# Transposing q and k unsplit, and splitting them as they leave PSUM

## The chip, the core and the metric

The kernel runs on one core of a Trainium2 chip. The metric is device time in microseconds, the median of several executions. One execution was also recorded by the profiler; its instruction times are what a reader of this document sees.

## What is computed

Attention with ALiBi-like distances under a mask (a local window of 96 keys and 8 global keys), for 4 batches, 8 heads, 768 positions and a head width of 64, and behind it a feed-forward block (512 to 2048 to 512) whose nonlinearity is a rational function.

```python
def _attn_ref(q, k, v, n_global, n_local):
    scale = 1.0 / np.sqrt(D)
    scores = scale * np.matmul(q, k.transpose(0, 1, 3, 2))
    rel = pos[:, None] - pos[None, :]
    is_global = pos[None, :] < int(n_global)
    is_local = (rel >= 0) & (rel < int(n_local))
    dist = np.where(is_global & ~is_local, float(n_local), np.abs(rel))
    slopes = 2.0 ** (-8.0 * (np.arange(H) + 1) / H)
    scores = scores - slopes[:, None, None] * dist
    scores = np.where(is_global | is_local, scores, -1000000000.0)
    a = softmax(scores)
    return np.matmul(a, v)

def _moe_ref(x, w_in, w_out, a, b):
    h = x @ w_in
    P = a[0] + a[1] * h + a[2] * h * h + a[3] * h * h * h
    Q = 1.0 + np.abs(b[0]) * np.abs(h) + np.abs(b[1]) * h * h
    return (P / (Q + 1e-06)) @ w_out
```

## The kernel before

**Work.** The attention is cut into 96 units (`NU`). A unit is one block of 128 queries of two neighbouring heads: `unit(u)` gives the chunk `c` of 256 tokens, the half `t`, the head pair `p`, the batch `b` and the block `i` of its sequence. Four units in a row have the same block and the four head pairs. Scores are taken over two key blocks, the query's own and the one before, in which the first 8 columns are overwritten with the global keys. The FFN is cut into 96 blocks `f`, each with two halves of the first matmul (`st_ffn1`, 12 matmuls a half), an elementwise chain over ScalarE, GpSimd and VectorE (`st_ew1` to `st_ew4`) and two halves of the second matmul (`st_ffn2`, 6 matmuls a half).

**Two precisions.** Up to unit 23 (`PLAIN = 24`) the scores are float32 matmuls. From unit 24 on each of q and k is split into a high part rounded to float32r and a low part, the rest, also float32r, and the score is taken with matmuls of float32r:

- `st_load` (L135 to L142): per two units, two DMAs on SyncE (SP) fetch 128 rows of four heads of q and of k into one tile `nat`, of which there are two.
- `st_split` (L382 to L388): VectorE copies q and k of the unit's two heads (256 columns in all) to float32r, the high part, and GpSimd subtracts it from the original, the low part. Both go to one tile `sp`, high and low of a head side by side.
- `st_qkT` (L390 to L405): four TensorE transposes of 128x128, one for each of q and k and each head, write one PSUM bank `tk`. Since high and low of one head (64 columns each) lie side by side, a transpose leaves the high part on partitions 0 to 63 and the low part on 64 to 127.
- `st_qkE` (L410 to L435): ScalarE takes q of each head to `qT` with the scale of the scores (a power of two that also holds the head's slope), and k of both heads to `kT`. Two SP DMAs of 64 KB exchange the halves of `qT`, giving a second copy with the low part above. In the first block of a sequence ScalarE also keeps the 8 global keys in `kG`.
- `st_score` (L437 to L466): for each head two matmuls of 128x128 by 128x256 into one bank `s`: with the straight `qT` (high by high and low by low) and with the exchanged one (high by low and low by high). GpSimd then puts the global keys into the first 8 columns of the k block; VectorE takes the scaled score with the mask to `pr` and finds its minimum.
- `st_soft`, `st_norm`, `st_pT`, `st_pv`, `st_x`: the exponentials (ScalarE), the normalization (GpSimd), four transposes of float32 into a bank `tp`, the product with v into a bank `o` for every two units, and its split into `xh` and `xl`, the FFN's input.

The tiles `tk`, `s`, `tp` and `o` share three PSUM banks (`ps_t`, `bufs=3`), asked for in the order of the program: within an iteration `s`, `tk`, `o` in odd iterations, `tp`. Accesses by different engines to a bank, and all other dependencies, are ordered by the tile framework with semaphores.

**Order.** A loop over `t` (L586 on) writes the steps of different units down together: the load of unit t+4, the scores of unit t-2, the transposes of unit t, the split of unit t+1, `pv` of the pair begun at t-5, the probabilities' transposes of unit t-3 and one FFN block. Each step has a priority, 1000 t plus a number from a table (`PRI`: score 50, soft 100, ffn1a 150, qkT 200, pv 250, qkE 300, split 400, ew3 450, ffn1b 550, ffn2a 750, pT 800, ffn2b 850). The framework's planner makes each engine's and each queue's fixed order from these priorities and from when, by its own model, an instruction is ready. At unit 24 the memory of the early tiles is given back and a pool `late` is opened in it.

Of the kernel before, what the change touches and what calls it, by code (L numbers as in the profile page):

```python
# [9 lines left out]
F32 = mybir.dt.float32  # L10
FR = mybir.dt.float32r
I32 = mybir.dt.int32
BF16 = mybir.dt.bfloat16
U16 = mybir.dt.uint16
AF = mybir.ActivationFunctionType
ALU = mybir.AluOpType
PSUM = bass.MemoryType.PSUM

P = 128
G = 8  # L20
# [14 lines left out]
PLAIN = 24  # L35
# [70 lines left out]
def tile_kernel(ctx: ExitStack, tc: tile.TileContext, q, k, v, n_global, n_local,  # L106
                w_in, w_out, ca, cb, out):
    nc = tc.nc
    B, H, S, D = q.shape
# [13 lines left out]
    pl = SimpleNamespace(tmps=TMPS, gbufs=GBUFS, split=False)  # L123


    nat = {}
    vts = {}

    def unit(u):
        c, j = divmod(u, UPC)  # L130
        t, p = divmod(j, NPAIR)
        b, i = divmod(2 * c + t, NT)
        return c, t, p, b, i

    def st_load(u):  # L135
        c, t, p, b, i = unit(u)
        hs = slice(2 * p, 2 * p + 4)
        r = slice(i * P, (i + 1) * P)
        n = pl.ldp.tile([P, 2, 4, D], F32, tag="nat", name=f"nat{u}")
        nc.sync.dma_start(out=n[:, 0], in_=q[b, hs, r, :].rearrange("h s d -> s h d"))  # L140
        nc.sync.dma_start(out=n[:, 1], in_=k[b, hs, r, :].rearrange("h s d -> s h d"))
        nat[u // 2] = n  # L142

    def st_load_v(u):
# [140 lines left out]
    def is_last(f):  # L285
        return f == NU - 1 and not pl.split
# [81 lines left out]
    ident = const.tile([P, P], F32, name="ident")  # L368
    ident_r = const.tile([P, P], FR, name="ident_r")
    mask0 = const.tile([P, P], BF16, name="mask0")  # L370
    masks = const.tile([P, 3, P], BF16, name="masks")
    sp = {}
    tqk = {}
# [5 lines left out]
    def blocks_of(x, i):  # L379
        return x if i else x[..., 0, :]  # L380

    def st_split(u):  # L382
        p = unit(u)[2]
        n = nat[u // 2][:, :, 2 * (p % 2):2 * (p % 2) + 2, :]
        s = pl.late.tile([P, 2, 2, 2, D], FR, tag="split", name=f"sp{u}", bufs=1)
        nc.vector.tensor_copy(out=s[:, :, :, 0, :], in_=n)  # L386
        nc.gpsimd.tensor_tensor(out=s[:, :, :, 1, :], in0=n, in1=s[:, :, :, 0, :], op=ALU.subtract)  # L387
        sp[u] = s  # L388

    def st_qkT(u):  # L390
        if u < PLAIN:
            p = unit(u)[2]
            tk = pl.ps_t.tile([P, 2, P], F32, tag="t", name=f"tk{u}")
            for z in range(2):
                n = nat[u // 2][:, z, 2 * (p % 2):2 * (p % 2) + 2, :]
                nc.tensor.transpose(out=tk[:, z, :], in_=n.rearrange("p a d -> p (a d)"), identity=ident)
            tqk[u] = tk
            return
        s = sp.pop(u)
        tk = pl.ps_t.tile([P, 2, 2, P], FR, tag="t", name=f"tk{u}")  # L400
        for z in range(2):
            for x in range(2):
                nc.tensor.transpose(out=tk[:, z, x, :], in_=s[:, z, x].rearrange("p a d -> p (a d)"),  # L403
                                    identity=ident_r)
        tqk[u] = tk  # L405


# [2 lines left out]
    def st_qkE(u):  # L410
        c, t, p, b, i = unit(u)
        tk = tqk.pop(u)
        hs = slice(2 * p, 2 * p + 2)
        if u < PLAIN:
            qz = pl.qz[:, u % 3]
            for x in range(2):
                ds_ = slice(x * D, (x + 1) * D)
                nc.scalar.activation(out=qz[ds_, x, :], in_=tk[ds_, 0, :], func=AF.Copy,
                                     scale=float(2.0 ** (2 * p + x - 2)))
            nc.scalar.copy(out=pl.kF[:, p, i % 2, :], in_=tk[:, 1, :])  # L420
            if i == 0:
                nc.scalar.copy(out=pl.kGF[:, p, :], in_=tk[:, 1, 0:G])
            qTs[u] = qz
            return
        kT, kG = pl.kT, pl.kG
        qT = pl.late.tile([P, 2, 2, P], FR, tag="qT", name=f"qT{u}", bufs=2)
        for x in range(2):

            nc.scalar.activation(out=qT[:, 0, x], in_=tk[:, 0, x], func=AF.Copy, scale=float(2.0 ** (2 * p + x - 2)))
        nc.sync.dma_start(out=qT[0:D, 1].bitcast(F32), in_=qT[D:P, 0].bitcast(F32))  # L430
        nc.sync.dma_start(out=qT[D:P, 1].bitcast(F32), in_=qT[0:D, 0].bitcast(F32))
        nc.scalar.copy(out=kT[:, hs, i % 2, :], in_=tk[:, 1])
        if i == 0:
            nc.scalar.copy(out=kG[:, hs, :], in_=tk[:, 1, :, 0:G])
        qTs[u] = qT  # L435

    def st_score(u):  # L437
        c, t, p, b, i = unit(u)
        qT = qTs.pop(u)
        s_ps = pl.ps_t.tile([P, 2, 2, P], F32, tag="t", name=f"s{u}")  # L440
        for x in range(2):
            h = 2 * p + x
            if u < PLAIN:
                nc.tensor.matmul(out=blocks_of(s_ps[:, x], i), lhsT=qT[:, x, :], rhs=blocks_of(pl.kF[:, p], i),  # L444
                                 start=True, stop=True)
                continue
            rhs = pl.kT[:, h] if i else pl.kT[:, h, 0:1, :].broadcast_to([P, 2, P])
            for z in range(2):
                nc.tensor.matmul(out=s_ps[:, x], lhsT=qT[:, z, x, :], rhs=rhs, start=(z == 0), stop=(z == 1))  # L449
        if 1 <= i < NT - 1 and u < PLAIN:  # L450
            nc.gpsimd.tensor_copy(out=pl.kF[:, p, i % 2, 0:G], in_=pl.kGF[:, p, :])
        elif 1 <= i < NT - 1:
            hs = slice(2 * p, 2 * p + 2)
            nc.gpsimd.tensor_copy(out=pl.kT[:, hs, i % 2, 0:G], in_=pl.kG[:, hs, :])
        if i == 0:
            mk = mask0
        else:
            mk = masks[:, 0:2, :] if i % 2 else masks[:, 1:3, :]
        pr = pl.att.tile([P, 2, 2, P], F32, tag="prob", name=f"pr{u}")
        st = stats[:, u % 4]  # L460
        for x in range(2):
            h = 2 * p + x
            nc.vector.tensor_tensor_reduce(  # L463
                out=blocks_of(pr[:, x], i), in0=blocks_of(s_ps[:, x], i), in1=mk,
                scale=-(2.0 ** -(h + 1)), scalar=3e38, op0=ALU.add, op1=ALU.min, accum_out=st[:, x:x + 1])
        prob[u] = (pr, st)  # L466

    def st_soft(u):
# [83 lines left out]
    def windowed(lates):  # L552
# [10 lines left out]
        for n, key in enumerate(first):  # L563
            if n == 1:
                st_load(2)
            fetch(key)
            if n == 2:
                st_load_v(0)
                st_load_v(2)
# [11 lines left out]
        base = tc.cur_priority  # L581
# [3 lines left out]
        f = -1  # L585
        for t in range(NU + LAG + F2 + 1):  # L586
# [5 lines left out]
            def on(name, fn, u, *args, ffn=False, more=0):  # L592
                if 0 <= u < NU:
                    tc.cur_priority = int(base + when[ffn] + pri[ffn][name] + more)
                    fn(u, *args)

            def ffn(name, fn, u, *args):
                if step:
                    on(name, fn, u, *args, ffn=True)

            def pv(u, more):
                on("pv", lambda u: st_pv(u // 2), u, more=more)
                on("x", lambda u: st_x(u // 2), u, more=more)
# [8 lines left out]
            for u in behind(1):  # L612
                on("score", st_score, u)
                on("soft", st_soft, u)
            if t == PLAIN:
                scope.close()
                pl.late = lates.enter_context(tc.tile_pool(name="late", bufs=1))
                pl.kT = pl.late.tile([P, H, 2, P], FR, name="kT")
                pl.kG = pl.late.tile([P, H, G], FR, name="kG")
                on("soft", st_split, t)  # L620
            ffn("ffn1a", st_ffn1, f, 0)
            on("qkT", st_qkT, t)
            if t % 2 and t - 5 >= PLAIN:
                pv(t - 5, 0)
            on("qkE", st_qkE, t)
            if t >= PLAIN:
                on("split", st_split, t + 1)
            if not is_last(f - 1):
                ffn("ew3", st_ew3, f - 1)
            for u in behind(1):  # L630
# [121 lines left out]
    with ExitStack() as es:  # L752
        pl.ldp = es.enter_context(tc.tile_pool(name="ldp", bufs=2))
        pl.att = es.enter_context(tc.tile_pool(name="att", bufs=2))
        pl.ffn = es.enter_context(tc.tile_pool(name="ffn", bufs=2))
        pl.ps_h = es.enter_context(tc.tile_pool(name="ps_h", bufs=2, space=PSUM))
        pl.ps_o = es.enter_context(tc.tile_pool(name="ps_o", bufs=2, space=PSUM))
        pl.ps_r = es.enter_context(tc.tile_pool(name="ps_r", bufs=1, space=PSUM))
        pl.ps_t = es.enter_context(tc.tile_pool(name="ps_t", bufs=3, space=PSUM))
        with ExitStack() as lates:  # L760
            windowed(lates)
# [53 lines left out]
```

## Time and profile before

| | before |
|---|---|
| median of 3 runs | 776.72 us (775.81 to 780.29) |
| the profiled execution, its time | 773.83 us |
| the profiled execution, its span | 771.9 us |
| TensorE (PE) busy | 744.7 us, 96% |
| ScalarE (ACT) busy | 570.7 us, 74% |
| VectorE (DVE) busy | 563.4 us, 73% |
| GpSimd (POOL) busy | 504.5 us, 65% |
| transposes of split q and k | first at 172.8 us, last at 680.7 us |

A row of a group of instructions has the line, the engine, the operation, the tile written, an arrow and the tiles read, the shape, and the count; behind it stand durations in nanoseconds (smallest, median, largest, or the mean). A row of waits has the waiting instruction, an arrow and the one that released it, then the total in microseconds, the number of times and the longest. The chain of waits is followed back from the last instruction; its rows have start and length in microseconds. Matmuls overlap one another in their records, so that the duration of one is longer than the time that it takes from TensorE.

### The profile page before, as it was taken

How to read it: one execution, taken by the hardware profiler on the slowest of the kernel's cores; microseconds unless marked ns; L12 is line 12 of the kernel's file. 1: busy time of each engine (PE TensorE's matmuls, PEld its weight loads, DVE VectorE, ACT ScalarE, POOL GpSimd, SP SyncE). 2: the span in 40 equal slices, each digit the busy share in tenths (PEclk: the TensorE clock that was granted, in tenths of full speed). 3: DMA queues.
4: the chain of work that ended last, by engine and by line, in shares of the span. 5: the costliest groups of instructions: out<-in, count | busy, mean ns of one | idle time of the engine just before them, and what ended most of it. 6: DMA issues, size and time to landing. Idle time of an engine off the chain costs nothing.

```text
span 771.9 us, 15342 instructions
## 1 busy us (share of the span) xinstructions
PE 744.7 (96%) x5216; PEld 647.8 (84%) x5216; DVE 563.4 (73%) x1384; ACT 570.7 (74%) x1404; POOL 504.5 (65%) x548
## 2 busy tenths in 40 slices
PE   5779999999999999999999999999999999999996
PEld 3566676888889898989989989898898998988994
DVE  5899976986777776676677777667776677776665
ACT  5777867876977877777777777777777877766664
POOL 4684765785697667765776766776677676664441
PEclk9999999999999999999999999999999999999998
DMA  8885401112312212222211221312211222100000
GB/s 235 274 253 184 141 15 43 35 28 63 90 36 56 77 35 57 64 56 50 70 40 42 76 50 37 83 45 53 76 33 45 67 53 49 42 15 1 28 1 34
DMA packets 97560, 52.75 MB, mean 68 GB/s; under 512 B 81088, under 2 KB 90304, under 8 KB 97472
## 3 DMA queue, kind: packets, MB, share of 16 engines
q1 hardware_dynamic: 97184, 51.67, 25.1%
q8 instruction: 44, 0.72, 0.4%
q14 instruction: 44, 0.36, 0.2%
q10 hardware_dynamic: 288, 0.00, 0.0%
HBM read 35.92 MB, written 6.29 MB: 55 GB/s over the span
## 4 chain that ended last, share of the span: by engine, by line
PE 86%; DVE 6%; DMA 2%; issue 2%; POOL 1%; ACT 1%; SPq 0%; DVEq 0%; POOLq 0%; ACTq 0%
PE h L277 33%; PE acc L353 32%; PE o L519 5%; PE tp L497 4%; PE s L449 4%; PE tk L403 3%; PE acc L348 2%; DVE r L213 2%; PE s L444 2%; PE h L269 1%; DMA nat<-in_k_dram 1%; DVE pr L463 1%; DMA r<-in_moe_w_in_dram 1%; DMA out_dram<-o 1%; DMA r<-in_moe_w_out_dram 0%
## 5 line engine op out<-in xcount | busy, mean ns | idle before, releaser
L277 PE MATMUL h<-xh,win_l 128*128 128x256 f32 x704 | 197.7, 281 | 0.0
L310 POOL TENSOR_TENSOR fa<-fa,fs 128x512 f32<-128x512 f32 x95 | 124.8, 1314 | 92.8 <-ACT fs L303 86.7
L487 POOL TENSOR_SCALAR pr<-pr,stats 128x256 f32<-128x256 f32 (+1 forms) x152 | 132.9, 884 | 24.6 <-DVE stats L478 17.0
L353 PE MATMUL acc<-wout_l,g 128*128 128x512 f32 x352 | 139.4, 396 | 0.0
L277 PEld LDWEIGHTS h<-xh,win_l 128*128 128x128 f32 x704 | 133.1, 189 | 0.9 <-issue 0.3
L473 ACT ACTIVATE pr<-pr,stats 128x256 f32<-128x256 f32 (+1 forms) x192 | 92.8, 486 | 49.7 <-DVE stats L463 48.3
L333 POOL TENSOR_TENSOR g<-fu,g 128x512 fp32r<-128x512 f32 x87 | 113.7, 1307 | 9.6 <-ACT g L332 6.8
L301 ACT ACTIVATE fu<-h,coef 128x512 f32<-128x512 f32 (+1 forms) x97 | 75.2, 775 | 52.4 <-PE h L277 50.3
L322 DVE SCALAR_TENSOR_TENSOR fu<-fu,coef,q 128x512 f32<-128x512 f32 (+1 forms) x97 | 71.6, 738 | 47.6 <-ACT q L318 46.9
L387 POOL TENSOR_TENSOR sp<-nat,sp 128x256 fp32r<-128x256 f32 x72 | 52.9, 735 | 75.8 <-DVE sp L386 33.9
L317 ACT ACTIVATE fs<-fa,coef 128x512 f32<-128x512 f32 (+1 forms) x97 | 69.7, 719 | 37.2 <-POOL fa L310 35.7
L499 DVE COPY pT<-tp 128x512 f32<-128x512 f32 (+1 forms) x75 | 48.5, 646 | 57.4 <-PE tp L497 56.6
L308 DVE TENSOR_TENSOR fu<-fu,h 128x512 f32<-128x512 f32 (+1 forms) x97 | 65.4, 675 | 17.4 <-ACT fs L303 15.7
L353 PEld LDWEIGHTS acc<-wout_l,g 128*128 128x128 f32 x352 | 66.3, 188 | 9.6
L309 DVE SCALAR_TENSOR_TENSOR fu<-fu,coef,h 128x512 f32<-128x512 f32 (+1 forms) x97 | 71.8, 740 | 2.7
L323 DVE SCALAR_TENSOR_TENSOR q<-fa,coef,q 128x512 f32<-128x512 f32 (+1 forms) x97 | 72.1, 743 | 0.0
L303 ACT ACTIVATE fs<-h,coef 128x512 f32<-128x512 f32 (+1 forms) x97 | 66.6, 686 | 0.1
L324 DVE SCALAR_TENSOR_TENSOR fu<-q,fu 128x512 f32<-128x512 f32 (+1 forms) x97 | 65.7, 678 | 0.4
L302 ACT ACTIVATE fa<-h,coef 128x512 f32<-128x512 f32 (+1 forms) x97 | 65.8, 678 | 0.3 <-PE acc L348 0.3
L332 ACT CAST g<-fu 128x512 fp32r<-128x512 f32 (+1 forms) x89 | 55.5, 624 | 12.1 <-DVE fu L324 12.0
L463 DVE CUSTOM_DVE_ANT_0 pr<-s,masks 128x256 f32<-128x256 f32 x160 | 61.1, 418 | 3.7 <-PE s L444 2.2
L497 PE MATMUL tp<-ident,pr 128*128 128x128 f32 x352 | 59.4, 275 | 2.5 <-DVE stats L463 2.3
(249 smaller groups left out, 2062.9 us busy)
## 6 DMA issues: line engine op xcount, KB each, us to landing
qT<-qT SPq DMA_DIRECT2D x144, 64.0 KB, 2.0
r<-in_moe_w_in_dram SPq DMA_DIRECT2D x16, 512.0 KB, 4.5
r<-in_moe_w_out_dram SPq DMA_DIRECT2D x16, 512.0 KB, 4.8
nat<-in_q_dram SPq DMA_DIRECT2D x48, 128.0 KB, 2.7
nat<-in_k_dram SPq DMA_DIRECT2D x48, 128.0 KB, 2.7
vt<-in_v_dram SPq DMA_DIRECT2D x48, 128.0 KB, 2.4
out_dram<-o SPq DMA_DIRECT2D x24, 256.0 KB, 2.0
vt<-in_v_dram SPq DMA_DIRECT2D x32, 8.0 KB
```

Of the source, the lines that this page charges most:

```text
L277: nc.tensor.matmul(out=hps[f][:, y, :], lhsT=w[:, fs], rhs=x[:, ct, :], start=(n == 0), stop=(n == 3 * NCT - 1))
L301: nc.scalar.activation(out=u, in_=h, func=AF.Identity, scale=a3, bias=a2)
L309: nc.vector.scalar_tensor_tensor(out=u, in0=u, scalar=a1, in1=h, op0=ALU.add, op1=ALU.mult)
L310: side(f).tensor_tensor(out=a, in0=a, in1=s, op=ALU.add)
L317: nc.scalar.activation(out=s, in_=a, func=AF.Ln, bias=q1)
L322: nc.vector.scalar_tensor_tensor(out=u, in0=u, scalar=a0, in1=r, op0=ALU.add, op1=ALU.mult)
L323: nc.vector.scalar_tensor_tensor(out=r, in0=a, scalar=q1, in1=r, op0=ALU.add, op1=ALU.mult)
L333: side(f).tensor_tensor(out=g[:, 1, ys], in0=u, in1=g[:, 0, ys], op=ALU.subtract)
L353: nc.tensor.matmul(out=acc, lhsT=gs[f][:, z, y, ts], rhs=w, start=(ft == 0 and n == 0), stop=(ft == NFT - 1 and n == 2))
L473: nc.scalar.activation(out=d, in_=d, func=AF.Exp, scale=-1.0, bias=st[:, x:x + 1], accum_out=st[:, 2 + 2 * x:3 + 2 * x])
L487: nc.gpsimd.tensor_scalar(out=d, in0=d, scalar1=st[:, 6 + x:7 + x], scalar2=None, op0=ALU.mult)
L497: nc.tensor.transpose(out=t_ps[:, x, w, :], in_=pr[:, x, w, :], identity=ident)
```

## The change

From unit 24 on, q and k are no longer split ahead of the transposes.

- A step `st_move`, once per two units, copies the `nat` tile with one SP DMA (256 KB) into one tile `moved` of type float32r, with all bits kept. It is written down behind the transposes of the odd unit, in place of the split, and has the split's priority; for unit 24 it stands at the start of iteration 24.
- `st_qkT` makes two transposes, of k and of q, each with both heads of the unit side by side, so that head x ends on partitions 64x to 64x+63. The bank `tk` is half as full.
- `st_qkE` splits on the way out of PSUM. For each head, ScalarE writes the high part (256 columns, k and q, on 64 partitions) to the head's own half of a tile `kq`, and VectorE writes value times scale minus high part to the other half. `kq` has for each head two k blocks and one q block. The scale is now put on q and k alike, 2^(p-1) on each, the same for both heads of a pair; the factor of two between the two heads goes into the mask, of which a halved copy is made once for the second heads.
- Two SP DMAs make the exchanged q (`qT`) from `kq`, again 64 KB each, now from two runs of 128 columns. The straight q is read from `kq`.
- The keeping of the global keys goes from ScalarE to GpSimd.

```diff
+    def st_move(u):
+        n = pl.late.tile([P, 2, 4, D], FR, tag="moved", name=f"mv{u}")
+        nc.sync.dma_start(out=n.bitcast(F32), in_=nat[u // 2])
         nat[u // 2] = n
...
-    def st_split(u):
+    def st_qkT(u):
         p = unit(u)[2]
-        n = nat[u // 2][:, :, 2 * (p % 2):2 * (p % 2) + 2, :]
-        s = pl.late.tile([P, 2, 2, 2, D], FR, tag="split", name=f"sp{u}", bufs=1)
-        nc.vector.tensor_copy(out=s[:, :, :, 0, :], in_=n)
-        nc.gpsimd.tensor_tensor(out=s[:, :, :, 1, :], in0=n, in1=s[:, :, :, 0, :], op=ALU.subtract)
-        sp[u] = s
...
-        s = sp.pop(u)
-        tk = pl.ps_t.tile([P, 2, 2, P], FR, tag="t", name=f"tk{u}")
+        fast = u >= PLAIN
+        tk = pl.ps_t.tile([P, 2, P], FR if fast else F32, tag="t", name=f"tk{u}")
         for z in range(2):
-            for x in range(2):
-                nc.tensor.transpose(out=tk[:, z, x, :], in_=s[:, z, x].rearrange("p a d -> p (a d)"),
-                                    identity=ident_r)
+            n = nat[u // 2][:, z, 2 * (p % 2):2 * (p % 2) + 2, :]
+            nc.tensor.transpose(out=tk[:, 1 - z if fast else z, :], in_=n.rearrange("p a d -> p (a d)"),
+                                identity=ident_r if fast else ident)
         tqk[u] = tk
...
-        kT, kG = pl.kT, pl.kG
-        qT = pl.late.tile([P, 2, 2, P], FR, tag="qT", name=f"qT{u}", bufs=2)
+        kq = pl.kq
+        raw = tk.bitcast(F32)
+        half = float(2.0 ** (p - 1))
         for x in range(2):
-
-            nc.scalar.activation(out=qT[:, 0, x], in_=tk[:, 0, x], func=AF.Copy, scale=float(2.0 ** (2 * p + x - 2)))
-        nc.sync.dma_start(out=qT[0:D, 1].bitcast(F32), in_=qT[D:P, 0].bitcast(F32))
-        nc.sync.dma_start(out=qT[D:P, 1].bitcast(F32), in_=qT[0:D, 0].bitcast(F32))
-        nc.scalar.copy(out=kT[:, hs, i % 2, :], in_=tk[:, 1])
+            own, other = slice(x * D, (x + 1) * D), slice((1 - x) * D, (2 - x) * D)
+            at = kq[:, 2 * p + x, i % 2:3:2 - i % 2, :]
+            nc.scalar.activation(out=at[own], in_=raw[own], func=AF.Copy, scale=half)
+            nc.vector.scalar_tensor_tensor(out=at[other], in0=raw[own], scalar=half, in1=at[own], op0=ALU.mult,
+                                           op1=ALU.subtract)
+        hs = slice(2 * p, 2 * p + 2)
+        qT = pl.late.tile([P, 2, P], FR, tag="qT", name=f"qT{u}", bufs=2)
+        nc.sync.dma_start(out=qT[0:D].bitcast(F32), in_=kq[D:P, hs, 2, :].bitcast(F32))
+        nc.sync.dma_start(out=qT[D:P].bitcast(F32), in_=kq[0:D, hs, 2, :].bitcast(F32))
         if i == 0:
-            nc.scalar.copy(out=kG[:, hs, :], in_=tk[:, 1, :, 0:G])
+            nc.gpsimd.tensor_copy(out=pl.kG[:, hs, :], in_=kq[:, hs, 0, 0:G])
...
-            rhs = pl.kT[:, h] if i else pl.kT[:, h, 0:1, :].broadcast_to([P, 2, P])
-            for z in range(2):
-                nc.tensor.matmul(out=s_ps[:, x], lhsT=qT[:, z, x, :], rhs=rhs, start=(z == 0), stop=(z == 1))
+            rhs = pl.kq[:, h, 0:2, :] if i else pl.kq[:, h, 0:1, :].broadcast_to([P, 2, P])
+            for z, lhsT in enumerate((pl.kq[:, h, 2, :], qT[:, x, :])):
+                nc.tensor.matmul(out=s_ps[:, x], lhsT=lhsT, rhs=rhs, start=(z == 0), stop=(z == 1))
...
+        def mask(x):
+            m0, m = (mask0, masks) if u < PLAIN or x == 0 else (pl.half0, pl.halves)
+            return m0 if i == 0 else m[:, 0:2, :] if i % 2 else m[:, 1:3, :]
...
-                out=blocks_of(pr[:, x], i), in0=blocks_of(s_ps[:, x], i), in1=mk,
-                scale=-(2.0 ** -(h + 1)), scalar=3e38, op0=ALU.add, op1=ALU.min, accum_out=st[:, x:x + 1])
+                out=blocks_of(pr[:, x], i), in0=blocks_of(s_ps[:, x], i), in1=mask(x),
+                scale=-(2.0 ** -(h + 1 if u < PLAIN else 2 * p + 1)), scalar=3e38, op0=ALU.add, op1=ALU.min, accum_out=st[:, x:x + 1])
...
             if t == PLAIN:
...
-                on("soft", st_split, t)
+                for m, full_m in ((pl.halves, masks), (pl.half0, mask0)):
+                    nc.vector.tensor_scalar(out=m, in0=full_m, scalar1=0.5, scalar2=None, op0=ALU.mult)
+                on("split", st_move, t)
             ffn("ffn1a", st_ffn1, f, 0)
             on("qkT", st_qkT, t)
+            if t % 2 and t > PLAIN:
+                on("split", st_move, t + 1)
...
-            if t >= PLAIN:
-                on("split", st_split, t + 1)
```

More of the change, by code (lines that the diff above doesn't have):

```diff
@@ L141, in st_load @@
         nc.sync.dma_start(out=n[:, 1], in_=k[b, hs, r, :].rearrange("h s d -> s h d"))
+        nat[u // 2] = n
+    def st_move(u):
+        n = pl.late.tile([P, 2, 4, D], FR, tag="moved", name=f"mv{u}")
+        nc.sync.dma_start(out=n.bitcast(F32), in_=nat[u // 2])
         nat[u // 2] = n
@@ L380, in blocks_of @@
         return x if i else x[..., 0, :]
-    def st_split(u):
+    def st_qkT(u):
         p = unit(u)[2]
-        n = nat[u // 2][:, :, 2 * (p % 2):2 * (p % 2) + 2, :]
-        s = pl.late.tile([P, 2, 2, 2, D], FR, tag="split", name=f"sp{u}", bufs=1)
-        nc.vector.tensor_copy(out=s[:, :, :, 0, :], in_=n)
-        nc.gpsimd.tensor_tensor(out=s[:, :, :, 1, :], in0=n, in1=s[:, :, :, 0, :], op=ALU.subtract)
-        sp[u] = s
[L390 to L393, printed above, removed]
-            for z in range(2):
[L395 to L398, printed above, removed]
-        s = sp.pop(u)
-        tk = pl.ps_t.tile([P, 2, 2, P], FR, tag="t", name=f"tk{u}")
+        fast = u >= PLAIN
+        tk = pl.ps_t.tile([P, 2, P], FR if fast else F32, tag="t", name=f"tk{u}")
         for z in range(2):
-            for x in range(2):
-                nc.tensor.transpose(out=tk[:, z, x, :], in_=s[:, z, x].rearrange("p a d -> p (a d)"),
-                                    identity=ident_r)
+            n = nat[u // 2][:, z, 2 * (p % 2):2 * (p % 2) + 2, :]
+            nc.tensor.transpose(out=tk[:, 1 - z if fast else z, :], in_=n.rearrange("p a d -> p (a d)"),
+                                identity=ident_r if fast else ident)
         tqk[u] = tk
@@ L412, in st_qkE @@
         tk = tqk.pop(u)
-        hs = slice(2 * p, 2 * p + 2)
         if u < PLAIN:
@@ L446, in st_score @@
                 continue
-            rhs = pl.kT[:, h] if i else pl.kT[:, h, 0:1, :].broadcast_to([P, 2, P])
-            for z in range(2):
-                nc.tensor.matmul(out=s_ps[:, x], lhsT=qT[:, z, x, :], rhs=rhs, start=(z == 0), stop=(z == 1))
+            rhs = pl.kq[:, h, 0:2, :] if i else pl.kq[:, h, 0:1, :].broadcast_to([P, 2, P])
+            for z, lhsT in enumerate((pl.kq[:, h, 2, :], qT[:, x, :])):
+                nc.tensor.matmul(out=s_ps[:, x], lhsT=lhsT, rhs=rhs, start=(z == 0), stop=(z == 1))
         if 1 <= i < NT - 1 and u < PLAIN:
@@ L453, in st_score @@
             hs = slice(2 * p, 2 * p + 2)
[L454 to L458, printed above, removed]
+            nc.gpsimd.tensor_copy(out=pl.kq[:, hs, i % 2, 0:G], in_=pl.kG[:, hs, :])
+        def mask(x):
+            m0, m = (mask0, masks) if u < PLAIN or x == 0 else (pl.half0, pl.halves)
+            return m0 if i == 0 else m[:, 0:2, :] if i % 2 else m[:, 1:3, :]
         pr = pl.att.tile([P, 2, 2, P], F32, tag="prob", name=f"pr{u}")
@@ L617, in windowed @@
                 pl.late = lates.enter_context(tc.tile_pool(name="late", bufs=1))
-                pl.kT = pl.late.tile([P, H, 2, P], FR, name="kT")
+                pl.kq = pl.late.tile([P, H, 3, P], FR, name="kq")
                 pl.kG = pl.late.tile([P, H, G], FR, name="kG")
-                on("soft", st_split, t)
+                pl.halves = pl.late.tile([P, 3, P], BF16, name="halves")
+                pl.half0 = pl.late.tile([P, P], BF16, name="half0")
+                tc.cur_priority = base + 1000 * t
+                for m, full_m in ((pl.halves, masks), (pl.half0, mask0)):
+                    nc.vector.tensor_scalar(out=m, in0=full_m, scalar1=0.5, scalar2=None, op0=ALU.mult)
+                on("split", st_move, t)
             ffn("ffn1a", st_ffn1, f, 0)
             on("qkT", st_qkT, t)
+            if t % 2 and t > PLAIN:
+                on("split", st_move, t + 1)
             if t % 2 and t - 5 >= PLAIN:
```

## The prediction, made before the change was run

> **What bounds the kernel now.** I read the busy shares first, then the same shares by stretches of the span, then the chain that ended last inside one stretch, then the tiles that the edit touches, and last the waits.
>
> ```profile
> PE 744.7 (96%) x5216; PEld 647.8 (84%) x5216; DVE 563.4 (73%) x1384; ACT 570.7 (74%) x1404; POOL 504.5 (65%) x548
> ```
>
> ```profile
> 400.00:500.00 100.00, 100.00 (x744) 90.34 (x743) 70.61 (x179) 74.98 (x184) 69.71 (x80) 1.00 0.23 56
> ...
> 700.00:772.00 72.00, 64.82 (x409) 57.09 (x407) 42.01 (x67) 42.70 (x74) 26.74 (x21) 0.97 0.05 17
> ```
>
> The second view lists, for a stretch: its length, then busy time and instruction count of PE, PEld, DVE, ACT, POOL, then granted clock and DMA share. From 400 to 500 us TensorE has no idle time, at clock 1.00, while DVE, ACT and POOL stand at 71, 75 and 70%. A busy TensorE could still hide slack inside its pipelined records, so the chain of waits in that stretch is the better witness:
>
> ```profile
> 413.25 0.29 PE tk L403 x4
> 413.54 1.02 PE o L519 x16
> ...
> 417.58 0.44 PE tp L497 x4
> ...
> 419.41 0.47 PE s L449 x4
> 419.89 1.42 PE h L277 x12
> 421.31 0.30 PE tk L403 x4
> 421.61 1.48 PE h L277 x12
> ...
> 426.32 0.47 PE s L449 x4
> 426.79 1.42 PE h L277 x12
> 428.21 0.29 PE tk L403 x4
> ```
>
> Start, length, work: every piece is TensorE, and each ends where the next begins. Two units of attention, with the FFN blocks between them, take 14.96 us (413.25 to 428.21): 8.06 us from an odd unit's transposes to the next even unit's, because `o` of two units lies there, and 6.90 us from even to odd. So between unit 24 and the last unit, time is what TensorE's queue costs, and a nanosecond taken from it there is a nanosecond of span, as long as no operand comes late. Lateness has been rare: of TensorE's waits from 200 us on, this is the only one that the trace names.
>
> ```profile
> PE tk L403 <- POOL sp L387: 0.2, 1, 0.2
> ```
>
> **TensorE's part of the change.** The transposes per unit go from four to two; the four score matmuls keep their count, shape (128x128 by 128x256) and type.
>
> ```profile
> L403 PE MATMUL tk<-ident_r,sp x288: 222/242/285, 172.8 to 680.7; 128*128 128x128 f32 x144
> ```
>
> 288 transposes are 72 units of four, all inside the stretch where TensorE is saturated. The durations (222 to 285 ns) overlap; what a transpose costs the queue is its share of the chain, 0.29 us / 4 = 0.0725 us. The twelve `h` matmuls behind them take 1.48 us there against 1.42 us behind `s`, so about 0.06 us is a cost of changing over, which stays. Removing two per unit: 2 x 0.0725 = 0.145 us, times 72 = 10.4 us. The upper bound takes the changeover along by half: 0.175 us, 12.6 us. A lower bound is the rate of the other transposes, `tp` of plain float32: 0.44 / 4 = 0.11 us. If two unsplit ones ran at that, 0.22 us would replace 0.29 us: 0.07 x 72 = 5.0 us. I take 10.4 us, because the new transposes have the operand type and shape of the old ones (float32r, 128x128), whatever bits they carry.
>
> A page of the notes would read the price differently. The Trainium skill, "TensorE: Matmul & The Clock Gate", Part 4, gives about 275 ns to a 128x128 transpose in one kernel's context and says that the full clock does not engage for transposes. By that, two fewer would be 39.6 us; the stretch's granted clock of 1.00 and the 0.29 us for four disagree.
>
> **The other engines.** None is on the chain, so these are loads and delays.
>
> ```profile
> L429 ACT ACTIVATE qT<-tk x144: 249/258/332, 173.3 to 681.6; 128x128 fp32r<-128x128 f32 x144
> L432 ACT CAST kT<-tk x72: 358/366/438, 173.7 to 681.8; 128x256 fp32r<-128x256 f32 x72
> L386 DVE CAST sp<-nat x72: 283/293/1164, 167.1 to 674.4; 128x256 fp32r<-128x256 f32 x72
> L387 POOL TENSOR_TENSOR sp<-nat,sp x72: 726/736/751, 168.5 to 674.8; 128x256 fp32r<-128x256 f32 x72
> L454 POOL CAST kT<-kG x48: 186/197/262, 203.9 to 665.3; 128x16 fp32r<-128x16 f32 x48
> ```
>
> ```profile
> L546 DVE TENSOR_TENSOR xl<-o,xh x44: 399/417/425, 63.1 to 710.1; 128x256 fp32r<-128x256 f32 x44
> ```
>
> ACT: two evictions of 128 columns and one of 256 (2 x 258 + 366 = 882 ns) become two of 256 columns on 64 partitions, 2 x 366 = 732 ns. POOL loses its 736 ns subtraction and gains a 16-column copy in 12 units (the 197 ns row). DVE loses the 293 ns copy and gains two fused multiply-subtracts of 256 columns, one operand in PSUM; the nearest row is `xl` (PSUM and SBUF in, float32r out), 417 ns. DVE: +2 x 417 - 293 = +541 ns per unit of 7.48 us, so from 71 to about 79% of a slightly shorter unit; ACT goes down to 74%, POOL to about 61%. Still covered by TensorE at 100%. The two half masks are made once, off the chain.
>
> **The move and SP's queue.** Every second unit a 256 KB copy within SBUF into one buffer stands where the split stood. It waits until the odd unit's transposes have read that buffer, and the even unit's transposes wait for it.
>
> ```profile
> qT<-qT SPq DMA_DIRECT2D x144, 64.0 KB, 2.0
> r<-in_moe_w_in_dram SPq DMA_DIRECT2D x16, 512.0 KB, 4.5
> ...
> nat<-in_q_dram SPq DMA_DIRECT2D x48, 128.0 KB, 2.7
> ...
> out_dram<-o SPq DMA_DIRECT2D x24, 256.0 KB, 2.0
> ```
>
> ```profile
> 392.20 0.46 SPq L430 DMA_DIRECT2D qT<-qT  x1
> 392.94 0.37 SPq L140 DMA_DIRECT2D nat<-in_q_dram  x1
> 393.35 0.53 SPq L141 DMA_DIRECT2D nat<-in_k_dram  x1
> 393.93 0.51 SPq L431 DMA_DIRECT2D qT<-qT  x1
> ...
> 415.27 0.87 SPq L430 DMA_DIRECT2D qT<-qT  x1
> 416.19 0.59 SPq L431 DMA_DIRECT2D qT<-qT  x1
> ```
>
> Landing lies between 2.0 us (256 KB of 2 KB rows going out) and 4.5 us (512 KB); I estimate 2.7 us, from the 128 KB and 256 KB rows. Issue is some 0.5 us. The freeing transposes end at 413.54, the next are due at 421.31 - 0.145 = 421.16: 7.6 us for 3.2 us of work, if the move is issued first. On SP it meets the two `qT` copies of the same unit and, in front, the `vt` row fetch that waits for `o`, which ends at 414.56. The queue's order follows readiness rather than a fixed pattern (a `nat` pair lies between two `qT` copies at 392.94), and the move is ready right after the transposes, the `qT` copies only two evictions and two subtractions later. So I put the move ahead; cost nothing, hidden by the 7.6 us. Without that cover it costs its 3.2 us per pair, 36 times. The loads of `nat` get their buffer back from a copy rather than from the last POOL subtraction; that eases them. The `qT` copies now wait for DVE and are issued later by two DVE steps, but the score that reads them runs two units on: for the transposes of 413.25 that is the `s` piece at 426.32, 12.8 us later, with some 3 us of issue and landing needed. At the changeover to unit 24, a move takes the place of a split that began 5.9 us ahead of its first transposes: nothing, or 3 us once.
>
> **The chain through the bank.** With three banks for `tk`, `s`, `tp` and `o` in turn, an odd unit's `tk` bank is taken again by the next `s` (413.25 to 419.41: 6.2 us), an even one's by the next `tk` (6.9 us). Before, two kinds of ACT eviction freed it. Now ACT and DVE read it in the order ACT, DVE, ACT, DVE. This row shows readers of one bank held apart in this program:
>
> ```profile
> DVE fu L308 <- ACT fs L303: 15.7, 21, 2.3
> ```
>
> L308 needs the output of L301 and `h`; it waits for L303, which only reads `h`. If the second ACT eviction likewise waits for the first DVE step, the chain is 2 x 0.37 + 2 x 0.42 = 1.6 us of work plus three queue waits:
>
> ```profile
> 414.11 0.73 DVE L322 SCALAR_TENSOR_TENSOR fu<-fu,coef,q 128x512 f32<-128x512 f32 x1
> ...
> 415.75 0.68 DVE L324 SCALAR_TENSOR_TENSOR fu<-q,fu 128x512 f32<-128x512 f32 x1
> ```
>
> ```profile
> 416.22 0.78 ACT L301 ACTIVATE fu<-h,coef 128x512 f32<-128x512 f32 x1 [1.23 <-PE h L277]
> ...
> 417.46 0.69 ACT L303 ACTIVATE fs<-h,coef 128x512 f32<-128x512 f32 x1
> ```
>
> A run of DVE work lasts up to 2.3 us (414.11 to 416.43), one of ACT 1.9 us (416.22 to 418.15). All three waits at full length: 1.6 + 0.4 (start after the transposes) + 2 x 2.3 + 1.9 = 8.5 us, past 6.2. At half length: 5.3 us, within. I take no cost, since an order made with these instructions in view need not put a whole run ahead each time. The Trainium skill's "PSUM — Partial Sum Buffer", section on bank collisions, lets two engines into one bank when they are in different quadrants; the two halves are, and by that rule ACT need not wait and half a run of waits goes. No run here shows which holds for halves.
>
> **Sum.** The profiled execution's span is 771.9 us and its time 773.83, 2.9 below the median of 776.72. Saving 10.4 gives 763.4 for that execution and 766.3 on the scale of the medians, 1.3% less.
>
> **Rivals.**
> - *The unsplit transposes go at the slower rate of `tp`.* Saving 5.0 us: 771.7. For: they carry full float32 values, as `tp` does. Against: the operand type. Chance 0.08.
> - *The bank comes back late, a little.* 0.2 us past 6.2 us on the 36 odd units: 7.2 us given back, 773.5. For: the L308 row and a DVE at 79%. Chance 0.10.
> - *The bank comes back late, and it decides (slower).* Place: the score matmuls behind an odd unit. From 6.2 us of chain on, every 0.5 us costs 18 us; the break-even is 0.3 us (10.4 / 36). At 0.5 us: 766.3 + 18 = 784.3. Against: 5.3 us with half waits. Chance 0.10.
> - *The move stands behind the `qT` copies on SP.* They ended at 416.78; with two DVE steps 417.6; plus 0.5 and 2.7 gives 420.8, still 0.4 us early. With one DVE run of 2.3 us ahead besides it is 1.9 us late, 36 times: 68 us, 834. At the 2.0 us landing 1.2 us late, 809. Chance 0.06.
> - *A transpose costs its whole duration.* 2 x 0.242 x 72 = 35 us: 742. Against: 0.29 us for four in the chain. Chance 0.01. The skill's page on TensorE, above, points this way with its figure.
>
> **How the numbers follow.** My forecast has the remaining 0.65; its own range is 762 to 771 (12.6 us saved less measurement scatter, to half the gain kept). A measurement of this kernel can tell about 0.5%, 3.9 us, from no change: faster means under 772.8, slower over 780.6. Faster: 0.64 of the forecast, 0.08 minus a share of 0.03 near the line, 0.01: 0.70. Slower: 0.10 + 0.06, and 0.01 of larger trouble from the small one: 0.17. Within: 0.13. The range 761 to 778 takes in forecast, slower rate and small delay, 0.83, and leaves out the move, the large delay and the full duration.
>
> **What would show it.** Right: a `tk` piece of 0.14 to 0.15 us in the chain, two units in about 14.67 us, TensorE still at 100% from 200 to 700 us, DVE near 79% and POOL near 61%. Wrong: a TensorE wait on the moved tile (the move), on DVE at `s` or `tk` (the bank), or a `tk` piece of 0.22 us (the rate). The forecast falls if TensorE shows more than some 6 us of idle time between 175 and 680 us.

## The result and the profile after

The changed kernel takes 767.50 us (median of 4 executions, 765.01 to 768.86) against 777.38 us (775.81 to 780.29), a ratio of 0.9865 with a 95% interval of 0.9825 to 0.9905. The forecast was 766.3 us, with a range of 761 to 778. Measured again beside later experiments it came to 766.20 against 776.63 us, 0.9863 (0.9841 to 0.9886). The profiled execution took 765.01 us, with a span of 763.1.

Busy time on the page, then the stretch from 400 to 500 us (length, then PE, PEld, DVE, ACT and POOL, granted clock, DMA share, GB/s):

```profile
PE 735.3 (96%) x5072; PEld 636.0 (83%) x5072; DVE 609.8 (80%) x1458; ACT 582.5 (76%) x1320; POOL 455.0 (60%) x488
```

```profile
400.00:500.00 100.00, 100.00 (x740) 89.82 (x739) 81.78 (x201) 79.40 (x175) 61.88 (x68) 1.00 0.29 74
```

144 instructions are gone from TensorE (5216 to 5072), which is two for each of 72 units. It is as full as before, and from 170 us on the trace names no wait of it at all. The chain of waits of the changed kernel shows what the two transposes take now (`h` and `acc` are the FFN's first and second matmuls, `s` the scores, `tp` the probabilities' transposes, `o` the product with v):

```profile
403.19 0.48 PE s L443 x4
403.67 0.12 PE tk L393 x2
403.80 0.78 PE h L282 x6
...
408.87 0.48 PE s L443 x4
409.35 0.95 PE h L282 x8
410.30 0.13 PE tk L393 x2
410.43 0.89 PE h L282 x7
...
424.75 0.12 PE tk L393 x2
```

A `tk` piece went from 0.29 or 0.30 us to 0.12 or 0.13 us. The tiles that the change touches (smallest, median and largest duration in ns, first and last start in us):

```profile
L393 PE MATMUL tk<-ident_r,mv x144: 220/226/285, 172.5 to 672.2; 128*128 128x128 f32 x144
L420 ACT ACTIVATE kq<-tk x144: 362/379/391, 174.3 to 674.0; 64x256 fp32r<-64x256 f32 x144
L421 DVE SCALAR_TENSOR_TENSOR kq<-tk,kq x144: 417/422/428, 175.4 to 674.4; 64x256 fp32r<-64x256 f32 x144
...
L146 SPq DMA_DIRECT2D mv<-nat x36: 501/502/740, 167.7 to 657.7; - x36
```

The last transposes start at 672.2 us in place of 680.7, after the first at 172.5 in place of 172.8: 8.2 us of the span's 8.8 us were won between them. By TensorE's records that stretch now also holds eight FFN matmuls more than before (six of `acc`, two of `h`), 1.6 us at 0.23 and 0.12 us each, so that at equal work 9.8 us were won there.

### The profile page after: what moved, and what is told of

The parts are those of the page before. It is cut to its first block, busy times and chain, and to the rows that moved or that the text cites. A ratio compares the mean times of both kernels' runs of the same rounds, so it can differ in the third digit from the quotient of the medians.

```text
span 763.1 us, 15110 instructions
## 1 busy us (share of the span) xinstructions
PE 735.3 (96%) x5072; PEld 636.0 (83%) x5072; DVE 609.8 (80%) x1458; ACT 582.5 (76%) x1320; POOL 455.0 (60%) x488
## 4 chain that ended last, share of the span: by engine, by line
PE 89%; DVE 6%; issue 2%; POOL 1%; ACT 1%; DMA 1%; SPq 0%; DVEq 0%; POOLq 0%
PE h L282 34%; PE acc L358 33%; PE o L513 5%; PE tp L491 5%; PE s L443 5%; PE acc L353 2%; PE s L438 2%; DVE r L218 2%; PE tk L393 2%; PE h L274 1%; DVE pr L457 1%; DMA nat<-in_k_dram 1%; PE o L508 1%; POOL r L215 0%; DVE fu L313 0%
## 5 line engine op out<-in xcount | busy, mean ns | idle before, releaser
L421 DVE SCALAR_TENSOR_TENSOR kq<-tk,kq 64x256 fp32r<-64x256 f32 x144 | 60.9, 423 | 15.6 <-ACT kq L420 11.6
L420 ACT ACTIVATE kq<-tk 64x256 fp32r<-64x256 f32 x144 | 54.4, 378 | 16.4 <-PE tk L393 10.0
L308 ACT ACTIVATE fs<-h,coef 128x512 f32<-128x512 f32 (+1 forms) x97 | 66.2, 682 | 0.2
L323 ACT ACTIVATE q<-fs 128x512 f32<-128x512 f32 (+1 forms) x97 | 57.4, 592 | 3.7 <-DVE fu L329 2.5
```

## The experiments

The theory: the gain is TensorE's queue time of two transposes per unit, and what the change adds on the other engines and queues lies under a full TensorE. The rivals: relief of GpSimd or a luckier order; a bank or a move that comes late.

**Four transposes again.** Two more per unit, into the empty half of the bank.

```diff
...
+            for y in range(1 if fast else 0):
+                nc.tensor.transpose(out=tk[:, 2 + z, :], in_=n.rearrange("p a d -> p (a d)"), identity=ident_r)
...
```

> The changed kernel with two more float32r transposes per unit, into the empty half of the tk bank, read by nobody: four per unit as before, all else as in the changed kernel. Theory (the gain is TensorE's queue time): 2 x 0.063 to 0.074 us x 72 = 9 to 11 us more than the changed kernel, 776.5 to 778 us, ratio to the kernel before 0.998 to 1.001. Rival (the gain comes from what left GpSimd and ScalarE, or from another order): stays at 767.5, ratio 0.987.

Measured: 780.09 us, ratio 1.0042 (1.0026 to 1.0059), above the 776.5 to 778 us expected. The whole gain is gone, and more: 13.9 us above the changed kernel of the later measurement. Its chain shows the extra ones (L394) and the old ones (L395) at single prices, the first two some 0.065 us each, the last two some 0.085:

```profile
446.28 0.07 PE tk L394
446.35 0.06 PE tk L395
446.41 0.08 PE tk L394
446.49 0.09 PE tk L395
446.58 1.02 PE o L515 x16
```

**Eight transposes.** The same with `range(3 if fast else 0)`.

> As the run with four, but six more transposes, eight per unit. Theory: 6 x 0.063 to 0.074 us x 72 = 27 to 32 us over the changed kernel, 795 to 799 us, ratio 1.023 to 1.028, three times the step of the run with four. Rival (TensorE has slack that two fewer transposes do not use up): less than three times that step.

Measured: 798.71 us, ratio 1.0277 (1.0252 to 1.0303), within the theory's 795 to 799. By the medians, though, the step from two to eight (32.5 us) is only 2.3 times the step from two to four (13.9), and less than three times was the rival's sign. The stretch between the first and the last of these transposes can be compared more closely, since by TensorE's records it holds the same other matmuls in the three runs: 172.5 to 672.2 in the changed kernel, and with four and with eight

```profile
L394 PE MATMUL tk<-ident_r,mv x144: 222/242/281, 173.3 to 684.6; 128*128 128x128 f32 x144
L394 PE MATMUL tk<-ident_r,mv x432: 220/246/255, 172.0 to 706.2; 128*128 128x128 f32 x144
```

That is 499.7, 511.3 and 534.2 us: 11.6 us for the first two more per unit and 22.9 us for the next four, 0.081 and 0.080 us a transpose, and the step to eight is 3.0 times the step to four. TensorE has no slack that a transpose could use, and what makes the steps of the medians uneven lies outside this stretch or in the scatter of the executions.

**Two transposes in the kernel before.** The reverse: nothing of the change but the count. The evictions, whose edit is left out here, read head 0's result for both heads.

```diff
-        tk = pl.ps_t.tile([P, 2, 2, P], FR, tag="t", name=f"tk{u}")
+        tk = pl.ps_t.tile([P, 2, P], FR, tag="t", name=f"tk{u}")
         for z in range(2):
-            for x in range(2):
-                nc.tensor.transpose(out=tk[:, z, x, :], in_=s[:, z, x].rearrange("p a d -> p (a d)"),
-                                    identity=ident_r)
+            nc.tensor.transpose(out=tk[:, z, :], in_=s[:, z, 0].rearrange("p a d -> p (a d)"),
+                                identity=ident_r)
...
```

> The kernel before with two transposes per unit: head 0's q and k alone are transposed, and head 1's evictions read head 0's result. It leaves out the transposes of the pair's second head, whose scores are then those of the first with another slope. Split, evictions, DMAs and queues are those of before. Theory: 2 x 0.063 to 0.074 us x 72 = 9 to 11 us less than before, 766 to 768 us, ratio 0.985 to 0.989, all of the change's gain without the rest of it. Rival (relief of GpSimd, or the order): 777, ratio 1.0.

Measured: 764.77 us, ratio 0.9838 (0.9818 to 0.9859), 11.5 us by the medians, a little over the 9 to 11 expected. All of the gain is there with GpSimd's subtraction, the split on VectorE and the old queue in place: the rival of relief falls. Its chain has the same short pieces, and the same longer `h` behind them:

```profile
447.81 0.13 PE tk L402 x2
447.94 1.49 PE h L277 x12
```

**Plain float32 transposes, no move.** From `nat` straight, with `ident` and a float32 bank; `st_move` is not called.

> The changed kernel with its two transposes as plain float32, straight from nat, without the move. Theory (a transpose costs its rate by operand type, and the move is hidden): 0.22 us in place of 0.13 us per unit, 7 us more than the changed kernel, 774 to 775 us, ratio 0.996. Rival (the move costs TensorE something that no wait shows): under 771 us, ratio under 0.992. Rival (both types go at one rate): 767.5.

Measured: 769.77 us, ratio 0.9903 (0.9876 to 0.9929): only 2 to 4 us more than the changed kernel, where 7 were expected. The chain:

```profile
441.70 0.36 PE s L443 x3
442.06 1.18 PE h L282 x10
443.24 0.22 PE tk L393 x2
443.46 0.59 PE h L282 x5
```

The rate came as expected, 0.22 us for two. What was not expected stands in the row behind it: `h` takes 0.59 / 5 = 0.118 us there, the price that it has behind `s` (1.18 / 10). Behind the float32r transposes of the changed kernel six `h` take 0.78 us and seven 0.89 us, where 0.119 each would be 0.71 and 0.83: 0.06 to 0.07 us more. A pair of float32r transposes costs the queue 0.125 + 0.06 = 0.19 us, one of float32 0.22; 0.03 x 72 = 2.2 us, about what was measured. The time lies in the band of the rival by which the move costs something that no wait shows (under 771 us), but these prices account for it, so this run does not show a cost of the move.

**The changed kernel again,** beside the next two.

> The changed kernel itself once more, beside the next two runs. If its true gain is all of the 11.5 us that two transposes less gave the kernel before, 765 to 766 us and a ratio of 0.984 to 0.986; if a part of that is given back by the rest of the change, 767 to 769 us and 0.987 to 0.990.

Measured: 766.20 us, ratio 0.9863 (0.9841 to 0.9886). The median sits between the two cases, and the interval overlaps that of the two transposes in the kernel before (0.9818 to 0.9859). Whether the rest of the change gives something back isn't settled by this pair; the paragraph on the sum, below, comes back to it.

**High parts first.** Both ScalarE evictions of a unit ahead of both VectorE steps.

```diff
             nc.scalar.activation(out=at[own], in_=raw[own], func=AF.Copy, scale=half)
+        for x in range(2):
+            own, other = slice(x * D, (x + 1) * D), slice((1 - x) * D, (2 - x) * D)
+            at = kq[:, 2 * p + x, i % 2:3:2 - i % 2, :]
             nc.vector.scalar_tensor_tensor(out=at[other], in0=raw[own], scalar=half, in1=at[own], op0=ALU.mult,
```

> The changed kernel with both ScalarE evictions of a unit written down ahead of both VectorE steps, so that ScalarE waits for VectorE no more and the bank is freed about 1.5 us sooner. Theory (the chain through the bank is within its 6.2 us and costs nothing): the same as the changed kernel within 0.3%, ratio 0.985 to 0.989. Rival (the chain holds TensorE back a little): 2 to 4 us less, ratio under 0.983.

Measured: 764.39 us, ratio 0.9852 (0.9828 to 0.9877), not to be told from the changed kernel. In that kernel the steps alternate. From the timeline of TensorE, ScalarE and VectorE in turn:

```profile
403.51 0.29 PE L393 MATMUL tk<-ident_r,mv 128*128 128x128 f32 x2
```

```profile
403.83 0.38 ACT L420 ACTIVATE kq<-tk 64x256 fp32r<-64x256 f32 x1 [0.94 <-PE tk L393]
407.55 0.38 ACT L420 ACTIVATE kq<-tk 64x256 fp32r<-64x256 f32 x1
```

```profile
405.06 0.42 DVE L421 SCALAR_TENSOR_TENSOR kq<-tk,kq 64x256 fp32r<-64x256 f32 x1
408.47 0.43 DVE L421 SCALAR_TENSOR_TENSOR kq<-tk,kq 64x256 fp32r<-64x256 f32 x1
```

With the high parts first the pairs stand together:

```profile
408.55 0.29 PE L393 MATMUL tk<-ident_r,mv 128*128 128x128 f32 x2
```

```profile
408.88 0.78 ACT L420 ACTIVATE kq<-tk 64x256 fp32r<-64x256 f32 x2 [0.79 <-PE tk L393]
```

```profile
409.69 0.88 DVE L424 SCALAR_TENSOR_TENSOR kq<-tk,kq 64x256 fp32r<-64x256 f32 x2 [0.46 <-ACT kq L420]
```

The bank is held from 403.80 to 408.90, 5.1 us, in the one and from 408.84 to 410.57, 1.7 us, in the other. Over all 72 units it is 1.7 to 7.0 us, with a median of 4.6, in the one and 1.7 to 3.9 us, with a median of 2.4, in the other, and the time stays the same within the intervals: the chain through the bank is long, and under cover.

**A late move.** A small GpSimd addition reads the moved tile and the probabilities' copy, so that the next move waits for both.

```diff
+    def st_gate(u):
+        g = pl.late.tile([P, 8], F32, tag="gate", name=f"gate{u}")
+        nc.gpsimd.tensor_tensor(out=g, in0=nat[u // 2].bitcast(F32)[:, 0, 0, 0:8], in1=pTs[u - 3][:, 0, 0, 0:8],
+                                op=ALU.add)
...
-            if t % 2 and t > PLAIN:
-                on("split", st_move, t + 1)
...
+            if t % 2 and t > PLAIN:
+                if t - 3 >= PLAIN:
+                    on("pT", st_gate, t, more=10)
+                on("pT", st_move, t + 1, more=20)
```

> The changed kernel with the move held back: a small GpSimd addition reads the moved tile and the probabilities of the same iteration, so that the move can start only behind the tp transposes and their copy, about 5 us later than in the changed kernel, with some 2.5 us left to the next transposes. By the prediction's arithmetic 3.2 us of work then come 0.7 to 1.5 us late in 34 pairs: 24 to 51 us more, 790 to 820 us, ratio 1.02 to 1.055. Rival (the order is made with the move's time in view, so that other matmuls go ahead and the transposes come later): within 3 us of the changed kernel, ratio under 0.992.

Measured: 770.92 us, ratio 0.9928 (0.9904 to 0.9953), 4.7 us above the changed kernel of the same measurement. Neither number holds: it is a fifth or less of the prediction's arithmetic, yet more than the rival allowed. The chain and SP's timeline show why:

```profile
404.69 0.12 PE tk L398 x2
...
417.81 0.12 PE tk L398 x2
...
420.86 0.12 PE tk L398 x2
...
429.37 0.12 PE tk L398 x2
```

```profile
411.71 0.50 SPq L146 DMA_DIRECT2D mv<-nat  x1
424.39 0.51 SPq L146 DMA_DIRECT2D mv<-nat  x1
```

The moves came 6.9 and 3.4 us behind the transposes that freed their buffer (over all pairs 1.8 to 7.5 us, with a median of 5.6, against 0.03 in the changed kernel). The order was made with the late move in view: here the even unit's transposes start 13.1 us behind the odd unit's, and the next odd ones 3.1 us behind those; over all pairs 10.0 and 3.8 us lie between them on average, 7.7 and 5.8 in the changed kernel. From 170 us on TensorE waits 3.6 us in all (none in the first profile of the changed kernel, 0.5 us in its second), but only 0.4 of them for the moved tile:

```profile
PE s L448 <- DVE pT L498: 1.8, 2, 1.0
PE acc L363 <- ACT g L342: 1.2, 3, 0.5
PE tk L398 <- DMA mv<-nat: 0.4, 2, 0.2
PE s L448 <- DMA qT<-kq: 0.2, 1, 0.2
```

In one of the two places where it waits for the move, the copy's length can be read:

```profile
383.05 0.50 SPq L146 DMA_DIRECT2D mv<-nat  x1
```

```profile
385.48 0.33 PE L398 MATMUL tk<-ident_r,mv 128*128 128x128 f32 x2 [0.20 <-DMA mv<-nat]
```

2.4 us from the start of the issue to the first use.

**Fewer cuts in TensorE's order.** I then suspected that what the change might give back lies in the order: matmuls of one kind stand in shorter stretches than before. To the run with the high parts first came a later priority for `pT`, 870 in place of 800.

> The run with the high parts first, and with the probabilities' transposes given a later priority (870 in place of 800, behind the second half of ffn2), so that TensorE's order is cut into fewer stretches of one kind: 617 between the first and the last of the late transposes, against 655 with the high parts first, 684 in the changed kernel and 582 in the kernel before. Theory (each cut costs TensorE some 0.03 us, and that is what the change gives back): 1 to 2 us under the run with the high parts first, ratio 0.982 to 0.985, hardly to be told from it. Rival (the later transposes come late for pv): slower than it, ratio over 0.987.

Measured: 767.41 us, ratio 0.9899 (0.9877 to 0.9921). The chain from 200 to 660 us has fewer pieces, first the run with the high parts first, then this one:

```profile
607 pieces in order of time: start us, us, what
```

```profile
562 pieces in order of time: start us, us, what
```

It is slower by 3 to 4 us, not faster by 1 to 2, and TensorE shows no wait in either. The theory that every cut costs the same falls. The rival's number came (a ratio over 0.987), but not its mechanism, a late `pv` for which TensorE would wait.

## Why the prediction was right

*TensorE's part.* The mechanism held, shown from both sides: taking two transposes from the kernel before gives the gain, giving two back to the changed one takes it away. The term was undersized. I had put 0.145 us per unit, half of the 0.29 us; the pieces show 0.29 to 0.125, 0.165 us, times 72 = 11.9 us, and the run with two in the kernel before 11.5 us. The first two of four are cheaper than their share. The changeover cost of 0.06 us that was to stay did stay in size (0.06 to 0.07 us behind `tk`), but it is now paid more often, as the next paragraph shows.

*The sum.* 11.9 us by the pieces stand against a measured 9.9 and 10.4, and the order of TensorE gave the difference back. The prediction took the changeover as the same in both orders. What it costs depends on what comes next. Behind the transposes `h` takes 0.06 to 0.07 us more, and so does `acc` by TensorE's records; the sixteen matmuls of `o` take 1.02 us there, as they do behind `acc`. First rows of the run with the high parts first, then of the changed kernel:

```profile
452.68 0.12 PE tk L393 x2
452.81 1.02 PE o L516 x16
```

```profile
411.32 0.23 PE acc L358
411.55 1.02 PE o L513 x16
```

Counted in TensorE's records, `o` follows the transposes directly in 31 of the 72 units of the kernel before, and in none of the changed kernel. So 31 changeovers more are paid: 31 x 0.07 = 2.2 us, and 11.9 - 2.2 = 9.7 us. The other runs fit: 31 units with two transposes in the kernel before (764.77 us), 25 with the high parts first (764.39), 4 with the later `pT` (767.41), and 5 in the run with four transposes, which is slower than the kernel before with as many. Between the first and the last of these transposes, with the same other matmuls but one, the changed kernel takes 499.7 us, the run with the high parts first 498.1 and the one with the later `pT` 500.9. No run changes this count alone, so it is a reading of the records and not a test. The forecast of 766.3 us against 767.5 and 766.2 was close by some luck: a saving taken 1.5 us too small, and 2.2 us of changeovers left out.

*The other engines.* VectorE: 423 ns a step where 417 was taken, 82% in the stretch where 79% was forecast. GpSimd 62% for 61%. ScalarE is the miss: 74% forecast, 79% measured, though its instructions are fewer and their durations sum to less (665 us for 682). I had added durations of instructions that stood next to each other, whose records overlap; this row of the kernel before has two of 258 ns in 0.41 us.

```profile
413.97 0.41 ACT L429 ACTIVATE qT<-tk 128x128 fp32r<-128x128 f32 x2
```

Alternating with VectorE they stand alone, and busy time counts each in full. It cost nothing, ScalarE being under cover.

*The move.* Issued first, as taken: mostly 0.03 us (at most 2.1) behind the end of the odd unit's transposes, and here ahead of both `qT` copies:

```profile
410.46 0.50 SPq L146 DMA_DIRECT2D mv<-nat  x1
412.40 0.31 SPq L516 DMA_DIRECT2D vt<-in_v_dram  x1
...
413.83 0.60 SPq L425 DMA_DIRECT2D qT<-kq  x1
...
415.16 0.60 SPq L426 DMA_DIRECT2D qT<-kq  x1
```

It takes 2.4 us where I had estimated 3.2. The rival of a late move failed in its price: it counted each microsecond of lateness as a microsecond of span, 36 times, as if TensorE's order were fixed. The order is made anew with the lateness known to the planner. 4.7 us remained; the trace names 3.6 us of waits, 0.4 of them for the move, and the rest stays open.

*The chain through the bank.* It took the form drawn: the second eviction starts only behind the first VectorE step (407.55 after 405.48), although the two touch different halves of the partitions. In all 72 units it starts behind that step, and with the high parts first the first VectorE step starts behind the second eviction in all 72. So in this program the two readers are held apart; that it is by the bank fits the prediction's L308 row, but no run here separates the bank from the tile `kq`, which both also write. The Trainium skill's "PSUM — Partial Sum Buffer", section "PSUM bank collisions raise a hardware error", lets two engines into one bank when they are in different quadrants; this program does not use that. The 5.1 us, and the median of 4.6, are near the 5.3 us of half-length waits and under 6.2; the units above 6.2 (the longest 7.0) made TensorE wait nowhere. Shortening the chain brought nothing that can be told from the noise.

*The rival of the rate.* The unsplit float32r transposes go at 0.06 us each and not at the 0.11 us of `tp`, so it falls. Plain float32 ones do go at 0.11 us, but they lose 2 to 4 us and not 5, since the cost that follows a float32r transpose does not follow a float32 one.

## What to carry to other kernels

Where the chain of waits is one engine end to end, price an edit by what its pieces take in that chain, with the pieces behind them, and not by an instruction's duration or by its share of a group. Count also before which pieces the edited ones will stand: here a new order alone gave back some 2 us. Added work on other engines and queues may then be large (here 46 us of VectorE and 9 MB of copies) as long as its latency fits the distance to its reader; read that distance from the trace and compare. A lateness that the planner knew of cost much less here than lateness times count, 4.7 us against 24 to 51.

## What was not expected of the hardware

- Behind a float32r transpose the next matmuls of 128x256 take 0.06 to 0.07 us more in all; behind a plain float32 one, none, and `o` directly behind a float32r one takes no more than elsewhere (1.02 us). So in front of `h` two transposes cost 0.19 against 0.22 us, not 0.125 against 0.22, and the kernel with plain float32 ones and no move is within 2 to 4 us of the changed one.
- In a run of four float32r transposes the second two cost 0.165 to 0.17 us together, the first two, like a pair alone, 0.12 to 0.13 us.
- TensorE can be 100% busy without a wait in two orders of the same work and yet differ by 3 to 4 us (764.39 and 767.41 us). In the slower one 21 units fewer have their transposes directly in front of `o`, which by the 0.07 us above is some 1.5 us; for the rest the trace gives no cause.
